# Attention and a two-layer ffn in one kernel: the switch to TensorE's written order at tile 39 instead of tile 45

## The chip, the cores and the metric

The kernel runs on one core of a Trainium2 chip. The metric is the device time of one execution in microseconds. The kernel before took 706.51 us (median of 3 runs, 705.92 to 706.59).

## What is computed

The reference is an attention with a learned position bias, followed by a two-layer ffn on its output (shapes: 4 batches, 8 heads, 576 positions, head size 64; ffn 512 to 2048 to 512):

```python
scores = scale * np.matmul(q, k.transpose(0, 1, 3, 2))
...
h = np.maximum(x @ w1 + b1, 0.0)
bias = h @ w2
scores = scores + bias.transpose(2, 0, 1)[None, :, :, :]
...
attn = np.exp(scores)
attn = attn / (np.sum(attn, axis=-1, keepdims=True) + 1e-09)
return np.matmul(attn, v).astype(np.float32)
...
h = x @ w_in
relu6 = np.clip(h + 3.0, 0.0, 6.0)
g = h * relu6 / 6.0
return (g @ w_out).astype(np.float32)
```

The bias depends on positions and head alone, so it is the same for all batches.

## The kernel before, in words

**Attention.** The work of attention is cut into 144 tiles. A tile is one batch, one pair of heads and up to 128 query rows of one head. The first 64 tiles cover the query rows 0 to 255 of all batches, four tiles a unit (one batch, one pair of heads); the other 80 cover the rest, five tiles a unit. Each pass n of the main loop writes `front(n)` (L935) and `back(n)`: for tile n the score matmuls of the next tiles (`qk_step`, tile `s_ps`, L552, two tiles at once for the tiles from 32 on), the bias added with the row maximum (`soft_max`, DVE, L564), the exponential (ACT, L575), the split of the probabilities into two halves of 16 bits (`hl`, ACT or POOL L118 or L124, then DVE L141), their transpose by a DMA of the SP queue (`at`, L640), and, five tiles later, the product with v (`pv_ps`, L711).

**Bias table.** The table comes in 36 groups of 16 rows. A group is four relus (`z_e`, DVE L851 or ACT L855), eight matmuls (`b_ps`, L868), an eviction by ACT (`bo`, L884) and a store to memory (L890), from where the tiles load it again.

**Ffn.** There are eight ffns, one for each batch and each half of the query rows; ffn(0, 0) is the first. Each is a generator of steps. Sixteen h steps of 12 matmuls each (`h_ps`, L786) are followed for each step by a relu on ACT (L776), a multiply on DVE (L769), a 16-bit copy on ACT (L763) and a subtraction on POOL (L765). Sixteen o steps of 12 matmuls each (`o_ps`, L809) follow, with one eviction by ACT (`ot`, L819) for every four. Of the first ffn the o steps also wait for w_out, which is unpacked on the chip.

**What sets the order.** Up to a switch, a scheduler sets the order of all engines' instructions. At the switch, `open_steady` (L1132) writes all that is left of ffn(0, 0), calls `open_banks` (L1126), and calls `keep_order("PE")` (L1099), after which TensorE's instructions stand as the program writes them. `open_banks` changes the PSUM places from three double places for `s` and two single ones for `w` to two and four (`open_psum`, L73). With the four `w` places the bias matmuls go to two `w` places instead of one `s` place, and their eviction becomes two instructions of 288 columns instead of one of 576 (`bias_mm` L859, `bias_out` L874). After the switch the main loop gives each tile a credit of 2.0 ffn steps (key `rf`; 1.55 in the second half, key `rf1`) and writes steps as long as there is credit. Between the end of ffn(0, 0) and the switch the credit is kept but no step is written, because of the condition `(phase < 2 or steady[0])` (L1192). Here is the switch and the way it is called:

```python
    def open_steady():
        nonlocal phase
        while phase < 2:
            ffn_step()
        open_banks()
        steady[0] = True
        keep_order("PE")
...
        if n == START:
            open_ffn()
...
        if n == SWITCH:
            open_steady()
        if late:
            qk_step(n + 1)
```

Of the kernel before, what the change touches and what calls it, by code (L numbers as in the profile page):

```python
# [24 lines left out]
NG = S // 16  # L25
CQ = 2.0 ** -25
VC = 5 * 128
CFG = {'z0': 'AD', 'gz': 12, 'z1': 'AD', 'gz2': 16, 'zeng': 'DDA', 'sg': 'P', 'wm1': 'A', 'wm2': 'RRAAAAAA', 'hl': 'AP', 'gl': 'PP', 'vm': 'A', 'g0': 8, 'rwi': 2.0, 'rw0': 0.3, 'rw1': 0.7, 'ro': 0.85, 'rb': 1.7, 'rf0': 1.3, 'rf': 2.0, 'rf1': 1.55, 'la': 6, 'gq': 2, 'gap': 0.0, 'wu': 8, 'act': 'o', 'g1': 2, 'w64': 5, 'rfo': 2.3, 'tv': 'A', 'pw': 0, 'po': 0, 'gr': 'AD', 'wb': 3, 'fb': 2, 'spn': 45, 'sw': 45, 'ws': 2, 'kn': 10, 'kw': 1, 'os': 11, 'ro2': 2.0, 'bo': 12, 'rb0': 1.5, 'psw': 99, 'xp': 0, 'mw': 2}
F64_BIAS = 2.0 ** -112
F64_MAX = float(np.uint32(0x0FEFFFFF).view(np.float32))  # L30

# [2 lines left out]
def attention_moe_kernel(  # L34
# [16 lines left out]
    nc = tc.nc  # L51
    cfg = CFG
    tc.cur_priority = 10000
# [30 lines left out]
    phase = 0  # L84
    out_open = [False, 0]
    steady = [False]
    four = [False]
    queue = []
# [820 lines left out]
    def bias_next():  # L909
        z, m, o, d = emitted  # L910
        z_group(z)
        bias_mm(m)
        emitted[0] += 1
        emitted[1] += 1
        if o < m:
            bias_out(o)
            emitted[2] += 1
            bias_store()
# [16 lines left out]
    def front(n):  # L935
        late = at(n + 1) and not direct(*tiles[n + 1])
        if at(n + 1) and not late:
            qk_step(n + 1)
        if at(n):
            soft_max(n)  # L940
        if n == START:
            open_ffn()
        if n == cfg["psw"]:
# [5 lines that stand above are left out]
        if unit_at(n - 6):  # L949
            x_low(*unit_at(n - 6))  # L950
        if at(n - 1):
            soft_norm(n - 1)
        if at(n - 2):
            soft_low(n - 2)
            if tiles[n - 2][2] in (1, 3, 5, 7, 8):
                freed[0] += 1
        if at(n):
            aux(n)
        if at(n - 3):
            soft_turn(n - 3)  # L960
        if unit_at(n - 5):
            pv_step(*unit_at(n - 5))
        while len(bt_t) - freed[0] < 4 and len(bt_t) < len(keys):
            k, b, p, i = keys[len(bt_t)]
            if k - n > (cfg["la"] if n > 3 else 2):
                break
            bias_until(128 * i + 128 if i < 2 else S)
            bt_t[b, p, i] = load_bias(b, p, i)
        if unit_at(n - 6) and unit_at(n - 6)[1] == PAIRS - 1:
            return unit_at(n - 6)[::2]  # L970
        return None

    def back(n):
        if unit_at(n - 5):
            x_high(*unit_at(n - 5))
        if at(n):
            soft_exp(n)
# [83 lines left out]
    def steps(gen, acc, rate):  # L1061
        acc[0] += rate
        while acc[0] >= 1.0:
            acc[0] -= 1.0
            next(gen, None)
# [28 lines left out]
    credit = 0.0  # L1094
# [4 lines left out]
    def keep_order(*names):  # L1099
        engines = {getattr(mybir.EngineType, e) for e in names}  # L1100
        in_order.enter_context(tc.manual_schedule(engines=engines))
# [40 lines left out]
    def out_step():  # L1142
        if next(gen_o, "end") == "end":
            return False
        out_steps[0] += 1
        return True

    def ffn_step():
        nonlocal phase
        r = next(queue[0], "end")  # L1150
        if r == "w2":
            phase = 1.5
        if r == "end":
            queue.pop(0)
            phase = 2
        return r != "end" and r != "w2"
# [9 lines left out]
    for n in range(-1, NT + 7):  # L1166
        for _ in range(cfg["g1"]):
            if emitted[0] < 16:
                bias_next()
        if n < 7:  # L1170
            next(gen_v, None)
        if n == cfg["spn"]:
            keep_order("SP")
        done = front(n)
        if phase == 0:
            steps(gen_w, aw, cfg["rw1"])
        else:
            ao[0] += cfg["ro"] if out_steps[0] < cfg["os"] else cfg["ro2"]
            while ao[0] >= 1.0:
                ao[0] -= 1.0  # L1180
                out_ready = not out_step()
        if phase and out_steps[0] >= cfg["bo"]:
            steps(gen_b, ab, cfg["rb"])
        if done is not None and done != (0, 0):
            b, u = done
            queue.append(ffn(b, u))
        if queue:
            if phase == 1.5 and not out_ready:
                credit = cfg["gap"]
            else:  # L1190
                credit += cfg["rf0"] if phase == 1 else cfg["rfo"] if phase < 2 else cfg["rf1" if unit_no[min(n, NT - 1)] >= 16 else "rf"]
            while credit >= 1.0 and queue and (phase < 2 or steady[0]):  # L1192
                if ffn_step():
                    credit -= 1.0
                if phase == 1.5 and not out_ready:
                    break
        back(n)
# [8 lines left out]
def _layout(q, k, v, w1, b1, w2, moe_w_in, moe_w_out):  # L1206
# [7 lines left out]
    qkd = _np.concatenate([kd, qd], axis=5).reshape(Bn, PAIRS, 2, 128, HALF + 256)  # L1214
    qkd = qkd.transpose(0, 1, 3, 2, 4).reshape(Bn, PAIRS, 128, 512 + S)[:CFG["fb"]]
    rows = _np.arange(128)[:, None] + 128 * _np.arange(5)[None, :]
# [44 lines left out]
```

## Time and profile before

| | us |
|---|---|
| median of 3 runs | 706.51 |
| the profiled execution, its own time | 703.41 |
| its span, first to last instruction | 701.6 |
| TensorE matmul busy | 643.9 (92%) |
| VectorE busy | 485.6 (69%) |
| ScalarE busy | 488.1 (70%) |
| GpSimd busy | 261.8 (37%) |
| granted TensorE clock, mean | 0.981 of 2.4 GHz |

Busy time is the union of an engine's instructions over the span. TensorE's is the largest, but it is an average over stages: what the change is worth has to be read in the stretch between the new place of the switch and the old one. The granted clock is a mean of two levels, 1.2 and 2.4 GHz.

### The profile page before, as it was taken

Reading aid. Unit: us, or ns where it says so; the run is one execution under the profiler, and the core shown is the slowest. Engines: PE = TensorE matmul, PEld = TensorE weight load, DVE = VectorE, ACT = ScalarE, POOL = GpSimd, SP = SyncE. Lnnn points to the kernel's source line nnn. Section 1 sums busy time; section 2 is a strip of 40 time slices with the busy share of each in tenths; the row PEclk is TensorE's granted clock in tenths of the full one; section 3 lists DMA queues with packets and bytes.
Section 4 is the critical chain, followed back from the end, with each engine's and each line's share of the span. In section 5 each row is a group of like instructions: output and inputs, shape, how many; then the busy total and the mean of one; then the engine's idle time right before and its main releaser. Section 6 shows DMA issues by size and latency. Waiting matters only on the chain. (4 is left out here: it accounts for less than half of the span.)

```text
span 701.6 us, 15111 instructions
## 1 busy us (share of the span) xinstructions
PE 643.9 (92%) x5558; PEld 455.8 (65%) x5558; DVE 485.6 (69%) x1157; ACT 488.1 (70%) x963; POOL 261.8 (37%) x322
## 2 busy tenths in 40 slices
PE   7687899775997999899899799999999999999998
PEld 2234456552673777687788688767777777777775
DVE  7989878899758577568778877887678767610310
ACT  7987778986846788678658866887578756721620
POOL 1112126765202443147435643564245522520420
PEclk9989999998999899999999999999999999999999
DMA  8899679644897938998899899978895877300000
GB/s 295 294 349 340 244 291 341 235 138 105 222 232 189 244 71 222 219 260 185 211 241 258 166 184 198 226 135 187 166 221 135 192 139 148 56 10 29 1 10 28
DMA packets 175738, 130.13 MB, mean 185 GB/s; under 512 B 137521, under 2 KB 144945, under 8 KB 174641
## 3 DMA queue, kind: packets, MB, share of 16 engines
q1 hardware_dynamic: 165872, 113.84, 64.9%
q10 hardware_dynamic: 9792, 15.34, 7.2%
q8 instruction: 43, 0.70, 0.4%
q14 instruction: 31, 0.25, 0.1%
HBM read 77.24 MB, written 15.34 MB: 132 GB/s over the span
## 5 line engine op out<-in xcount | busy, mean ns | idle before, releaser
L786 PE MATMUL h_ps<-x,wi 128*128 128x256 f16 (+1 forms) x1536 | 200.1, 288 | 6.8 <-DVE x L141 3.3
L809 PE MATMUL o_ps<-g,wo 128*128 128x256 f16 (+1 forms) x1536 | 196.0, 286 | 1.1 <-POOL g L765 1.1
L786 PEld LDWEIGHTS <-wi 128*128 128x128 f16 x1536 | 147.9, 98 | 55.3 <-issue 12.9
L809 PEld LDWEIGHTS <-wo 128*128 128x128 f16 x1536 | 147.2, 98 | 47.7 <-issue 10.6
L765 POOL TENSOR_TENSOR g<-t,g 128x256 f16<-128x256 f32 (+1 forms) x128 | 104.2, 825 | 123.6 <-ACT g L763 122.9
L575 ACT ACTIVATE bt<-bt,sm 128x576 f32<-128x576 f32 x144 | 110.9, 771 | 53.2 <-DVE sm L564 51.6
L141 DVE SCALAR_TENSOR_TENSOR hl<-bt,sm,hl 128x576 f16<-128x576 f32 x112 | 99.7, 902 | 27.6 <-ACT hl L124 15.0
L769 DVE SCALAR_TENSOR_TENSOR t<-t,t,h_ps 128x320 f32<-128x320 f32 (+1 forms) x112 | 56.2, 516 | 66.0 <-ACT t L776 64.7
L118 POOL TENSOR_SCALAR hl<-bt,sm 128x576 f16<-128x576 f32 x56 | 46.7, 834 | 94.4 <-DVE sm L587 39.2
L763 ACT ACTIVATE g<-t 128x256 f16<-128x256 f32 (+1 forms) x128 | 55.6, 441 | 35.5 <-DVE t L769 34.6
L418 POOL TENSOR_TENSOR qkl<-st,qkh 128x576 fp32r<-128x576 f32 (+2 forms) x48 | 61.1, 1293 | 38.0 <-ACT qkh L411 31.0
L564 DVE CUSTOM_DVE_ANT_0 bt<-s_ps,bt 128x576 f32<-128x576 f32 x88 | 64.6, 751 | 14.4 <-PE s_ps L552 7.9
L776 ACT ACTIVATE t<-h_ps,t,hr 128x320 f32<-128x320 f32 (+1 forms) x112 | 64.6, 588 | 8.6 <-PE h_ps L786 6.9
L868 PE MATMUL b_ps<-z_e,w_sb 128*32 128x288 f32 x448 | 47.2, 440 | 17.0 <-POOL x L699 7.5
L819 ACT ACTIVATE ot<-o_ps,os 128x256 f32<-128x256 f32 (+1 forms) x32 | 16.0, 499 | 56.5 <-PE o_ps L809 55.6
L124 ACT ACTIVATE hl<-bt,sm 128x576 f16<-128x576 f32 x56 | 43.1, 772 | 10.5 <-issue 3.0
L583 DVE TENSOR_SCALAR sm<-sm 128x1 f32<-128x1 f32 x112 | 16.8, 150 | 41.2 <-ACT bt L575 41.2
L851 DVE TENSOR_SCALAR z_e<-T,nbp 128x576 f32<-128x576 f32 x69 | 38.8, 608 | 2.6 <-PE b_ps L868 2.5
L868 PEld LDWEIGHTS b_ps<-z_e,w_sb 128*32 128x32 f32 x448 | 15.4, 114 | 37.4 <-DVE z_e L851 8.0
L552 PE MATMUL s_ps<-qkh 64*128 64x288 f32 x192 | 30.0, 349 | 8.3 <-ACT bo L884 5.0
L855 ACT ACTIVATE z_e<-T,bp 128x576 f32<-128x576 f32 x43 | 32.4, 770 | 6.8 <-PE b_ps L868 3.1
L258 POOL TENSOR_SCALAR w<-w 128x1024 f32<-128x1024 f32 x8 | 11.5, 1441 | 64.0 <-ACT wo L257 57.9
(132 smaller groups left out, 908.6 us busy)
## 6 DMA issues: line engine op xcount, KB each, us to landing
bt<-bias SPq DMA_DIRECT2D x36, 576.0 KB, 5.7
bias<-bo ACTq DMA_DIRECT2D x36, 288.0 KB, 5.4
w<-in_w_in_dram SPq DMA_DIRECT2D x8, 1024.0 KB, 7.1
vs<-in_vp_dram SPq DMA_DIRECT2D x24, 320.0 KB, 5.4
st<-in_qk_dram SPq DMA_DIRECT2D x16, 448.0 KB, 4.5
wo<-in_w_out_dram SPq DMA_DIRECT2D x5, 1024.0 KB, 6.4
bt<-bias SPq DMA_DIRECT2D x16, 288.0 KB, 3.5
qk<-in_qkd_dram SPq DMA_DIRECT2D x8, 544.0 KB, 8.9
```

Of the source, the lines that this page charges most:

```text
L118: nc.gpsimd.tensor_scalar(out=out, in0=full, scalar1=scale, scalar2=1.0, op0=ALU.mult, op1=ALU.mult)
L141: nc.vector.scalar_tensor_tensor(out=out, in0=full, scalar=scale, in1=high, op0=ALU.mult, op1=ALU.subtract)
L418: nc.gpsimd.tensor_sub(out=lo[:, c:c + w], in0=t[:, c:c + w], in1=hi[:, c:c + w].bitcast(F32))
L564: nc.vector.tensor_tensor_reduce(out=halves(bt), in0=ps, in1=halves(src), op0=ALU.add, op1=ALU.min, scale=-0.125, scalar=3.0e38, accum_out ...
L575: nc.scalar.activation(out=bt, in_=bt, func=AF.Exp, scale=-1.0, bias=sm[:, 0:1], accum_out=total)
L763: nc.scalar.activation(out=g[:, 0], in_=uu, func=AF.Copy)
L765: e.tensor_sub(out=g[:, 1], in0=uu, in1=g[:, 0])
L769: nc.vector.scalar_tensor_tensor(out=t_t[f], in0=t_t[f], scalar=cols(f)[2], in1=h_t.pop(f)[:, 0:n], op0=ALU.min, op1=ALU.mult,)
L776: nc.scalar.activation(out=t_t[f], in_=h_t[f][:, 0:n], func=AF.Relu, scale=cols(f)[0], bias=cols(f)[1],)
L786: nc.tensor.matmul(out=h_t[f][:, 0:n], lhsT=wi[:, a, c, f * 128:(f + 1) * 128], rhs=x[:, e, c], start=(k == 0), stop=(k == 3 * KC - 1),)
L809: nc.tensor.matmul(out=ops[:, 0:n], lhsT=wo[:, a, f, e * 128:(e + 1) * 128], rhs=g_t[f][:, r], start=(f == 0 and a == 0 and r == 0), stop= ...
L868: nc.tensor.matmul(out=pss[a][32 * k:32 * k + 32, 0:HALF], lhsT=w2_sb, rhs=z[:, a * HALF:(a + 1) * HALF],)
```

## The change

One number of the table at the top, `sw`, goes from 45 to 39. It is `SWITCH`, the tile at which `open_steady` is called. A new key `he` is 0, so the condition that names it is what it was.

```diff
-CFG = {... 'spn': 45, 'sw': 45, 'ws': 2, ... 'mw': 2}
+CFG = {... 'spn': 45, 'sw': 39, 'ws': 2, ... 'mw': 2, 'he': 0}
...
-            while credit >= 1.0 and queue and (phase < 2 or steady[0]):
+            while credit >= 1.0 and queue and (phase < 2 or steady[0] or cfg["he"]):
```

The number moves instructions on all engines but SP, whose order stays the same row for row. The first place is TensorE around the scores of tiles 44 to 47. Before, these rows stand there (`b_ps` is a group of the bias table, `m_ps` a step of the scale of v, `s_ps` the scores; a row's last number is how many follow each other):

```order
L868 MATMUL b_ps<-z_e,w_sb 32x288 x7
L157 MATMUL m_ps<-g_v_2299,ones_sb 128x1
L552 MATMUL s_ps<-qkh 128x288 x2
L552 MATMUL s_ps<-qkl,qkh 128x288 x2
L552 MATMUL s_ps<-qkh,qkl 128x288 x2
L868 MATMUL b_ps<-z_e,w_sb 32x288 x16
L552 MATMUL s_ps<-qkh 128x288 x4
L552 MATMUL s_ps<-qkl,qkh 128x288 x4
L552 MATMUL s_ps<-qkh,qkl 128x288 x4
L868 MATMUL b_ps<-z_e,w_sb 32x288 x8
L786 LDWEIGHTS wi
L786 MATMUL h_ps<-x,wi 128x256
```

Nothing of an ffn stands between the scores of tiles 44 and 45 (three rows of two matmuls, the second half of a pair that the scheduler had split) and those of 46 and 47 (three rows of four). The last row is the first of 120 matmuls of `h_ps`, ten steps that are written at once. With the change, the scores of a pair stand so (this is tiles 42 and 43, the rows of the following pairs are alike):

```order
L786 LDWEIGHTS wi
L786 MATMUL h_ps<-x,wi 128x256
L552 MATMUL s_ps<-qkh 128x288 x4
L552 MATMUL s_ps<-qkl,qkh 128x288 x4
L552 MATMUL s_ps<-qkh,qkl 128x288 x4
L153 MATMUL m_ps<-eye_sb,m_v_2275 1x128
L868 MATMUL b_ps<-z_e,w_sb 32x288 x8
L786 LDWEIGHTS wi
L786 MATMUL h_ps<-x,wi 128x256
```

The h steps of ffn(1, 0) now stand in pieces of 24 matmuls between the scores, the bias groups and the products with v, from the pair of tiles 40 and 41 on. Between the last o step that both orders share and the scores of tiles 48 and 49, TensorE had 84 matmuls of `o_ps`, the scores of four pairs, seven bias groups, two products with v and 144 matmuls of `h_ps`; it now has the same with 192 of `h_ps`. From there to the end the new order is 48 ffn matmuls ahead of the old one at the same tile (60 at some tiles), and after the last product with v 528 of them are left instead of 576.

The second place is ScalarE, which evicts and converts for all of these. Before, around the same tiles (`vh` is a half of v, `qkh` a half of q and k):

```order
L124 ACTIVATE vh<-vs,s_v_1309 128x640
L890 DMA bias_99<-bo 16x8x576
L124 ACTIVATE hl<-bt,sm 128x576
L855 ACTIVATE z_e<-T,bp 128x576
L884 ACTIVATE bo<-b_ps,cv_sb,isc 128x576
L890 DMA bias_100<-bo 16x8x576
L411 ACTIVATE qkh<-st 128x832
L575 ACTIVATE bt,sm<-bt,sm 128x576
L884 ACTIVATE bo<-b_ps,cv_sb,isc 128x288
```

And with the change:

```order
L884 ACTIVATE bo<-b_ps,cv_sb,isc 128x288
L575 ACTIVATE bt,sm<-bt,sm 128x576
L776 ACTIVATE t<-h_ps,t_1745,hr_2230 128x256
L890 DMA bias_99<-bo 16x8x576
L884 ACTIVATE bo<-b_ps,cv_sb,isc 128x288
L776 ACTIVATE t<-h_ps,t_1745,hr_2230 128x256
L124 ACTIVATE hl<-bt,sm 128x576
L855 ACTIVATE z_e<-T,bp 128x576
L884 ACTIVATE bo<-b_ps,cv_sb,isc 128x288
L855 ACTIVATE z_e<-T,bp 128x576
L763 ACTIVATE g<-t 128x256
L776 ACTIVATE t<-h_ps,t_1745,hr_2230 128x256
```

The relus and copies of the h steps (L776, L763) now stand among the evictions of the bias groups, which come in halves of 288 columns. In all, 32 evictions are halves instead of 22, and 20 are whole instead of 25.

## Rows read from the trace of the kernel before

**Rows 1.** The chain that ended last, in order of time: start, us, what.

```profile
460.56 1.06 PE s_ps L552 x7
...
617.87 2.02 PE pv_ps L711 x28
...
672.16 26.09 PE o_ps L809 x192
```

**Rows 2.** Windows: length, busy us of PE, PEld, DVE, ACT, POOL; clock, DMA, GB/s.

```profile
197.27:251.03 53.76, 47.27 (x451) 34.33 (x447) 34.49 (x83) 36.99 (x70) 15.40 (x20) 0.94 0.78 205
...
251.03:311.90 60.87, 58.74 (x627) 43.90 (x628) 41.25 (x97) 45.95 (x93) 19.10 (x24) 1.00 0.86 202
...
311.77:334.00 22.23, 20.76 (x217) 17.25 (x217) 17.86 (x43) 19.02 (x45) 14.66 (x20) 1.00 0.84 203
```

**Rows 3.** Timeline of TensorE, 218 to 234 us: start, us, what [idle before <-releaser].

```profile
218.71 1.94 PE L868 MATMUL b_ps<-z_e,w_sb 128*32 128x288 f32 x16
222.17 2.02 PE L868 MATMUL b_ps<-z_e,w_sb 128*32 128x288 f32 x16 [1.53 <-DVE z_e L851]
224.12 0.40 PE L552 MATMUL s_ps<-qkh 64*128 64x288 f32 x1
229.48 0.84 PE L552 MATMUL s_ps<-qkh 64*128 64x288 f32 x3 [4.97 <-ACT bo L884]
...
231.22 2.15 PE L868 MATMUL b_ps<-z_e,w_sb 128*32 128x288 f32 x16
233.29 13.98 PE L786 MATMUL h_ps<-x,wi 128*128 128x256 f16 x120
```

**Rows 4.** Timeline of all engines, ScalarE's rows before 229 us.

```profile
227.26 0.78 ACT L124 ACTIVATE hl<-bt,sm 128x576 f16<-128x576 f32 x1 [2.14 <-DMA at<-hl]
...
228.62 0.81 ACT L884 ACTIVATE bo<-b_ps,cv_sb,isc 128x576 f32<-128x576 f32 x1
```

**Rows 5.** Timeline of TensorE, 199 to 217 us, without waits.

```profile
199.99 0.53 PE L552 MATMUL s_ps<-qkh 64*128 64x288 f32 x4
...
200.98 1.18 PE L868 MATMUL b_ps<-z_e,w_sb 128*32 128x288 f32 x16
202.09 5.41 PE L809 MATMUL o_ps<-g,wo 128*128 128x256 f16 x48
207.43 1.17 PE L711 MATMUL pv_ps<-at,vh 128*64 128x256 f16 x18
...
209.09 1.48 PE L809 MATMUL o_ps<-g,wo 128*128 128x256 f16 x12
...
212.59 0.27 PE L153 MATMUL m_ps<-eye_sb,m_v 128*1 128x128 f32 x1
...
215.05 0.53 PE L552 MATMUL s_ps<-qkh 64*128 64x288 f32 x2
...
216.03 1.40 PE L868 MATMUL b_ps<-z_e,w_sb 128*32 128x288 f32 x14
```

**Rows 6.** Window of ffn(1, 0)'s h steps before, columns as in rows 2.

```profile
233.29:262.33 29.04, 29.04 (x296) 23.15 (x293) 19.12 (x43) 24.29 (x53) 12.96 (x20) 0.97 0.57 145
```

**Rows 7.** ScalarE's groups by line in that window: xcount | busy us, mean ns.

```profile
L884 ACT ACTIVATE bo<-b_ps,cv_sb,isc 128x288 f32<-128x288 f32 x6 | 3.5, 582 | 0.0
L855 ACT ACTIVATE z_e<-T,bp 128x576 f32<-128x576 f32 x4 | 3.1, 770 | 0.0
L575 ACT ACTIVATE bt<-bt,sm 128x576 f32<-128x576 f32 x3 | 2.3, 769 | 0.3 <-DVE sm L564 0.3
L124 ACT ACTIVATE hl<-bt,sm 128x576 f16<-128x576 f32 x2 | 1.5, 766 | 0.0
...
L124 ACT ACTIVATE vh<-vs,s_v 128x640 f16<-128x640 f32 x1 | 0.8, 832 | 0.1
```

**Rows 8.** Windows of 10 us: the one with ScalarE's largest share after 250 us.

```profile
390.00:400.00 10.00, 8.10 (x87) 6.58 (x87) 8.50 (x19) 9.37 (x22) 7.72 (x10) 1.00 0.67 134
```

**Rows 9.** Timeline of TensorE, the longest wait of a bias group after 250 us.

```profile
291.31 1.17 PE L868 MATMUL b_ps<-z_e,w_sb 128*32 128x288 f32 x12 [2.13 <-ACT z_e L855]
```

More of the change, by code (lines that the diff above doesn't have):

```diff
@@ L27 @@
 VC = 5 * 128
-CFG = {'z0': 'AD', 'gz': 12, 'z1': 'AD', 'gz2': 16, 'zeng': 'DDA', 'sg': 'P', 'wm1': 'A', 'wm2': 'RRAAAAAA', 'hl': 'AP', 'gl': 'PP', 'vm': 'A', 'g0': 8, 'rwi': 2.0, 'rw0': 0.3, 'rw1': 0.7, 'ro': 0.85, 'rb': 1.7, 'rf0': 1.3, 'rf': 2.0, 'rf1': 1.55, 'la': 6, 'gq': 2, 'gap': 0.0, 'wu': 8, 'act': 'o', 'g1': 2, 'w64': 5, 'rfo': 2.3, 'tv': 'A', 'pw': 0, 'po': 0, 'gr': 'AD', 'wb': 3, 'fb': 2, 'spn': 45, 'sw': 45, 'ws': 2, 'kn': 10, 'kw': 1, 'os': 11, 'ro2': 2.0, 'bo': 12, 'rb0': 1.5, 'psw': 99, 'xp': 0, 'mw': 2}
+CFG = {'z0': 'AD', 'gz': 12, 'z1': 'AD', 'gz2': 16, 'zeng': 'DDA', 'sg': 'P', 'wm1': 'A', 'wm2': 'RRAAAAAA', 'hl': 'AP', 'gl': 'PP', 'vm': 'A', 'g0': 8, 'rwi': 2.0, 'rw0': 0.3, 'rw1': 0.7, 'ro': 0.85, 'rb': 1.7, 'rf0': 1.3, 'rf': 2.0, 'rf1': 1.55, 'la': 6, 'gq': 2, 'gap': 0.0, 'wu': 8, 'act': 'o', 'g1': 2, 'w64': 5, 'rfo': 2.3, 'tv': 'A', 'pw': 0, 'po': 0, 'gr': 'AD', 'wb': 3, 'fb': 2, 'spn': 45, 'sw': 39, 'ws': 2, 'kn': 10, 'kw': 1, 'os': 11, 'ro2': 2.0, 'bo': 12, 'rb0': 1.5, 'psw': 99, 'xp': 0, 'mw': 2, 'he': 0}
 F64_BIAS = 2.0 ** -112
```

## The prediction

> **What bounds the kernel now.** I read the chain of waits first. From 460 us to the end it is TensorE alone, with hardly a gap: the scores at 460.56, the last product with v at 617.87, then only ffn matmuls, the last 192 of them in 26.09 us [rows 1]. So whatever TensorE does not get done before 460 us is paid at the end, at full price, and a microsecond that TensorE loses before then is a microsecond of the total. The question is how much it loses where the change works.
>
> The windows answer this. Between the last o step that both orders share (197.27 us) and the scores of tiles 48 and 49 (251.03 us) lie 53.76 us, of which TensorE is busy 47.27; the mean granted clock is 0.94, so part of it runs at 1.2 instead of 2.4 GHz. In the 60.87 us behind it TensorE idles 2.13 us, and the clock is 1.00 [rows 2]. The timeline shows the place: a bias group waits 1.53 us for VectorE's `z_e`, then the second score matmul of tiles 46 and 47 waits 4.97 us for ScalarE's eviction `bo`, because bias group and scores share the three `s` places; the rows after it take about twice their price until 233.29, where 120 matmuls of `h_ps` follow [rows 3]. ScalarE itself was late there: it stood 2.14 us before `hl`, for a transpose by DMA, with `bo` queued two instructions behind [rows 4]. TensorE had nothing else to do, as its order holds no ffn work between tiles 44 and 47.
>
> **The change, step by step.** First the prices, as distances between starts: the scores of a pair 0.99 us (199.99 to 200.98), a bias group 1.11, 48 matmuls of `o_ps` 5.34 (0.111 each), a product with v 1.66, a step of the v scale 0.27 [rows 5]; 120 matmuls of `h_ps` take 13.98, 0.1165 each [rows 3].
>
> *What TensorE must do in the stretch.* Before: 84 o matmuls 9.35, four pairs of scores 3.96, seven bias groups 7.77, two products with v 3.32, two small matmuls 0.54, 144 h matmuls 16.78; the sum is 41.7. It took 53.76 [rows 2], so 12.0 us are lost: 6.5 idle, and the rest the low clock and a pair of scores that the scheduler had split, whose half alone takes 0.98 (215.05 to 216.03) [rows 5]. With the change the same list has 192 h matmuls, 5.6 us more, 47.3 in all: without any wait, tiles 48 and 49 would be reached at 244.6 instead of 251.0, with 48 ffn matmuls more behind them. At the end, 48 matmuls less are left, 6.5 us by the last 192 (26.09 / 192 = 0.136 each) [rows 1]. Both are one gain: the total falls by what of the 12.0 us is no longer lost.
>
> *What is lost anew in that stretch: 5.0 us.* The h steps now run beside the bias groups, and ScalarE serves both. From the first h matmul (197.27 + 9.35 + 0.99 + 1.11 = 208.7) to 244.6 TensorE has 35.9 us of work. Before, the same sixteen h steps stood in a window of 29.04 us in which ScalarE was busy 24.29 [rows 6]. Counted in the order, the new stage has beside these 8 more half evictions (4.7 us at 582 ns), 4 more `z_e` (3.1), 5 more exponentials (3.8), 2 more `hl` (1.5) and 3 more conversions of the size of `vh` (2.5) [rows 7]. That makes 39.9 us of ScalarE for 35.9 of TensorE, so it falls 4.0 behind even if it never waits. The lower bound of the loss is the share that TensorE idles in the window after 251.03, 2.13 of 60.87, which is 1.3 us [rows 2]; the upper one is the densest 10 us of ScalarE, 9.37 busy, where TensorE gets 8.10 [rows 8]: 35.9 / 0.81 is 44.3, a loss of 8.4. I take 5.0, nearest the deficit itself.
>
> *What moves on from there: 1.0 us.* Two bias groups now fall into the h steps of the next ffn, which had none. That stage is 22.23 us with ScalarE at 19.02 [rows 2]; two groups are four half evictions and two or three `z_e`, 4.2 us, so 23.2 us, a deficit of 1.0. The bounds are 0 (ScalarE catches up in the o steps that follow) and 4.2.
>
> *Edits counted at nothing.* SP's order does not move. The reset of the PSUM places costs nothing that the order shows: it comes behind the drained o steps, whose last eviction is ScalarE's alone, and the next scores need only places that were read long before. If that cover is gone, it is one eviction, under 1 us. The two `s` places make a pair of scores wait for both row maxima of the pair before; with h steps between the pairs that is hidden, as it is after 251.03 now. Scores of tiles 40 and 41 start 60 o matmuls later than before (6.7 us), which hurts only if attention becomes the bound; it is ahead again by tiles 48 and 49.
>
> The sum is 12.0 - 5.0 - 1.0 = 6.0 us. Against the profiled execution, whose own time is 703.41 for a span of 701.6, that gives a span of 695.6 and an own time of 697.4. The median of the runs, 706.51, lies 3.1 above the profiled one; I carry the difference over: **700.5 us**.
>
> **The rivals.** A change under 1.4 us (0.2%) can't be told from none.
>
> *ScalarE takes the hole back.* If it sets the pace of the whole stage as in the densest 10 us, the loss is 8.4 us and the next stage adds 2.0, the middle of its bounds: 706.5 - 1.6 = 704.9, and 707.1 with 4.2 for the next stage. For it: the 39.9 against 35.9 above. Against: ScalarE has little to do during the o steps before 208, and its order puts relus between the bias rows. In this direction points a rule of the Trainium skill, "Perfetto Trace Analysis", section "Identifying the Most-Contended Engine": judge TensorE by its weight loads' share and not by matmul time, and take the engine with the highest share as the one to work on. By it the h window reads 23.15 for weight loads and 24.29 for ScalarE of 29.04 [rows 6], so ScalarE is the bound there and another order of TensorE gains nothing: 706.5. The trace speaks against it in that window, since TensorE's matmuls fill all 29.04.
>
> *Slower: a wait at each bias group.* TensorE's written order is rigid: behind each group's eight matmuls stand 24 h matmuls that can't pass it. After 250 us one group waited 2.13 us for ScalarE's `z_e` [rows 9]. If all seven in the stretch do, 14.9 us are lost where 12.0 were, and with the 1.0 of the next stage the time is 706.5 + 3.9 = 710.4. It decides from a mean of 1.6 us a group, (12.0 - 1.0) / 7. For it: relus and copies now stand ahead of `z_e` on ScalarE. Against: nine groups stand in the 60.87 us after 251.03, in written order, and all idle time of TensorE there is 2.13 us [rows 2].
>
> *The hole is filled for nothing.* ScalarE keeps up and TensorE loses as little as after 251.03, or later waits shrink as well: up to 12.0 us less, 694.5.
>
> *The change doesn't do what it says.* The credit could have been spent elsewhere; but the order shows the 48 matmuls ahead from tile 48 to the end. It would be 706.5.
>
> **How the numbers follow.** The forecast, 696.5 to 703.5, gets 0.62: the hole is in rows, its cause (no ffn work there) goes, and the deficit of ScalarE is smaller than the hole. The hole taken back gets 0.16, of which 0.09 lies below 705.1 and 0.07 about 706.5; the hole for nothing 0.13; slower 0.07; no effect 0.02. So faster is 0.62 + 0.13 + 0.09 = 0.84, the same 0.07 + 0.02 = 0.09, slower 0.07. The range is 696.0 to 705.0: the forecast and the near halves of the two cases beside it, with the dearest ScalarE loss (8.4 us and little behind it) still in it.
>
> **What would show it.** Right: no wait of TensorE over 3 us between 197 and 250 us, and the clock near 1.00 there; the scores of tiles 48 and 49 about 1.4 us earlier, near 249.6; ScalarE over 90% busy between 209 and 249, with short waits of `h_ps` and `b_ps` for ScalarE or VectorE that add up to some 5 us; the last product with v within 1 us of 617.9, and 528 ffn matmuls instead of 576 behind it, 6.5 us less. Wrong: a new wait of several us in the stretch, followed by rows at twice their price, or an idle time after 251.03 that grows by more than 2 us, which would mean that attention and not TensorE sets the pace.

## The result, and the profile after

| | before | changed |
|---|---|---|
| median, us | 706.55 (6 runs, 705.24 to 707.76) | 698.59 (6 runs, 696.51 to 700.03) |
| profiled execution, own time | 703.41 | 696.51 |
| its span | 701.6 | 694.5 |
| granted TensorE clock, mean | 0.981 | 0.990 |

The ratio is 0.9887, with a 95% interval of 0.9862 to 0.9912: the change makes the kernel 8.0 us faster. Forecast were 700.5 us, in a range of 696.0 to 705.0.

In the first part of the changed kernel's page the busy times of VectorE, ScalarE and GpSimd are those of before within 0.5 us; TensorE's matmuls have 5.7 us less (643.9 before):

```profile
PE 638.2 (92%) x5558; PEld 453.0 (65%) x5558; DVE 485.6 (70%) x1157; ACT 487.7 (70%) x968; POOL 261.7 (38%) x322
```

No matmul was taken away. So the gain has to be looked for in waits, and in matmuls that ran at the higher clock. The windows of the changed kernel answer to [rows 2]; columns as there.

```profile
200.96:251.92 50.96, 48.52 (x499) 36.08 (x495) 36.48 (x87) 40.26 (x83) 18.43 (x24) 1.00 0.73 199
251.92:311.90 59.98, 57.81 (x619) 43.32 (x619) 41.15 (x95) 44.46 (x92) 19.10 (x25) 1.00 0.95 214
```

The first window is the stretch of the prediction, from the last shared o step to the scores of tiles 48 and 49. It is 2.8 us shorter than before (53.76) and holds 48 more matmuls of the ffn, which are worth 5.6 us. TensorE idles 2.4 us in it instead of 6.5, and the clock is 1.00 instead of 0.94. The second window is much as before: 2.17 us idle, where it was 2.13.

TensorE's timeline, 200 to 252 us, against [rows 3] and [rows 5] (start, us, what, idle before and its releaser in brackets):

```profile
200.96 9.34 PE L809 MATMUL o_ps<-g,wo 128*128 128x256 f16 x84
210.23 0.53 PE L552 MATMUL s_ps<-qkh 64*128 64x288 f32 x4
...
212.33 2.79 PE L786 MATMUL h_ps<-x,wi 128*128 128x256 f16 x24
...
226.13 0.69 PE L868 MATMUL b_ps<-z_e,w_sb 128*32 128x288 f32 x8 [0.38 <-DVE p_v L160]
...
245.38 2.30 PE L868 MATMUL b_ps<-z_e,w_sb 128*32 128x288 f32 x16 [0.28 <-ACT z_e L855]
249.21 2.78 PE L786 MATMUL h_ps<-x,wi 128*128 128x256 f16 x24 [1.52 <-DVE t L769]
251.92 0.54 PE L552 MATMUL s_ps<-qkh 64*128 64x288 f32 x4
```

The wait of 4.97 us before the scores of tiles 46 and 47 is gone; nothing waits longer than 1.52. The waits that the profile lists for TensorE in this stretch, by what ended them (total us, times, longest):

```profile
PE h_ps L786 <- DVE t L769: 1.5, 1, 1.5
PE b_ps L868 <- DVE p_v L160: 0.4, 1, 0.4
PE b_ps L868 <- ACT z_e L855: 0.3, 1, 0.3
PE h_ps L786 <- ACT bo L884: 0.3, 1, 0.3
```

The chain that ended last, its tail, against [rows 1] (start, us, what):

```profile
617.23 2.02 PE pv_ps L711 x28
619.25 19.67 PE o_ps L809 x144
638.92 26.08 PE h_ps L786 x192
665.00 26.09 PE o_ps L809 x192
```

The last product with v starts at 617.23, where it was 617.87, and behind it stand 144 + 192 + 192 = 528 ffn matmuls instead of 576. Here the gain reaches the end of the kernel: 48 matmuls less, 6.5 us, plus the 0.64.

### The profile page after: what moved, and what is told of

Read it like the earlier page. It is cut to its first block, busy times and chain, and to the rows that moved or that the text cites. A ratio compares the mean times of both kernels' runs of the same rounds, so it can differ in the third digit from the quotient of the medians.

```text
span 694.5 us, 15117 instructions
## 1 busy us (share of the span) xinstructions
PE 638.2 (92%) x5558; PEld 453.0 (65%) x5558; DVE 485.6 (70%) x1157; ACT 487.7 (70%) x968; POOL 261.7 (38%) x322
## 5 line engine op out<-in xcount | busy, mean ns | idle before, releaser
L141 DVE SCALAR_TENSOR_TENSOR hl<-bt,sm,hl 128x576 f16<-128x576 f32 x112 | 99.1, 896 | 20.8 <-POOL hl L118 12.8
L763 ACT ACTIVATE g<-t 128x256 f16<-128x256 f32 (+1 forms) x128 | 55.4, 439 | 36.3 <-DVE t L769 35.5
L418 POOL TENSOR_TENSOR qkl<-st,qkh 128x576 fp32r<-128x576 f32 (+2 forms) x48 | 58.5, 1238 | 37.5 <-ACT qkh L411 30.3
L776 ACT ACTIVATE t<-h_ps,t,hr 128x320 f32<-128x320 f32 (+1 forms) x112 | 64.3, 586 | 7.2 <-PE h_ps L786 2.9
L868 PE MATMUL b_ps<-z_e,w_sb 128*32 128x288 f32 x448 | 45.4, 430 | 15.3 <-POOL x L699 5.9
L851 DVE TENSOR_SCALAR z_e<-T,nbp 128x576 f32<-128x576 f32 x69 | 40.9, 638 | 1.9 <-PE b_ps L868 1.7
L884 ACT ACTIVATE bo<-b_ps,cv_sb,isc 128x288 f32<-128x288 f32 (+1 forms) x52 | 35.0, 674 | 4.3 <-DMA bias<-bo 2.4
```

What stands on the lines that cost most here:

```text
L141: nc.vector.scalar_tensor_tensor(out=out, in0=full, scalar=scale, in1=high, op0=ALU.mult, op1=ALU.subtract)
L418: nc.gpsimd.tensor_sub(out=lo[:, c:c + w], in0=t[:, c:c + w], in1=hi[:, c:c + w].bitcast(F32))
L763: nc.scalar.activation(out=g[:, 0], in_=uu, func=AF.Copy)
L776: nc.scalar.activation(out=t_t[f], in_=h_t[f][:, 0:n], func=AF.Relu, scale=cols(f)[0], bias=cols(f)[1],)
L868: nc.tensor.matmul(out=pss[a][32 * k:32 * k + 32, 0:HALF], lhsT=w2_sb, rhs=z[:, a * HALF:(a + 1) * HALF],)
```

## The experiments

Two theories stood against each other at first. **Filling**: the gain comes from ffn work that stands between attention's matmuls in the stretch, so that TensorE has something to do while a bias group waits for its relus. **Places** or **order**: it comes from the PSUM places or from TensorE's written order, which the change also moves to tile 39. The first four runs take the change apart. For each run I work out from its profile what its stretch lost: its length, less the work in it by the prices of [rows 5] and [rows 3] (41.7 us with 144 h matmuls, 47.3 with 192). Before it was 12.0 us.

**Only the PSUM places at tile 39** (the key `psw` calls `open_banks` there; the rest of the switch stays at 45):

```diff
-'sw': 45, ... 'psw': 99
+'sw': 45, ... 'psw': 39
```

> Edit: only the PSUM places change at tile 39 (two double, four single); TensorE's written order and the further ffns still open at tile 45. Filling theory (the gain comes from h steps that stand where TensorE had nothing to do): no ffn work moves, so 705.0 to 708.0, and a stretch without ffn work between the scores of tiles 44 and 48 is still there. Places theory (the 4.97 us wait for the eviction of a bias group in a shared place was the loss): that wait goes, about 5 us and the low clock behind it come back, 698.5 to 701.5.

Measured: 708.89 us beside 706.68, ratio 1.0031 (1.0010 to 1.0052), slightly slower, and 0.9 above the range of the filling theory. TensorE's timeline in its stretch, with one row of ScalarE:

```profile
232.35 0.65 PE L868 MATMUL b_ps<-z_e,w_sb 128*32 128x288 f32 x2 [0.73 <-DVE z_e L851]
...
234.87 0.77 ACT L124 ACTIVATE hl<-bt,sm 128x576 f16<-128x576 f32 x1 [2.44 <-DMA at<-hl]
...
237.32 2.14 PE L868 MATMUL b_ps<-z_e,w_sb 128*32 128x288 f32 x14 [4.33 <-ACT z_e L855]
239.40 14.02 PE L786 MATMUL h_ps<-x,wi 128*128 128x256 f16 x120
```

The hole is still there, 4.33 us, though the bias group no longer shares places with the scores. It waits for the relu `z_e` now. So the three shared `s` places, which the prediction named as the hole's cause, were only the place where the lateness showed: with nothing of the ffn to do, TensorE meets the bias groups' relus and evictions wherever they are late. Lost: 13.7 us. The lateness itself begins further up, at the same place as before [rows 4]: ScalarE stood 2.44 us before `hl`, for a transpose by DMA, and this `z_e` was queued behind it. In the changed kernel's stretch ScalarE has no such wait. No run moves the transposes alone, so what makes them late is open.

**Only the written order from tile 39:**

```diff
+        if n == 39:
+            keep_order("PE")
...
     def open_steady():
...
-        keep_order("PE")
```

> Edit: only TensorE's written order begins at tile 39; places and further ffns at tile 45. Filling theory: no ffn work moves, but the pair of scores that the scheduler had split is whole again (1.0 us), so 704.5 to 707.5, with the hole between the scores of tiles 44 and 48. Order theory (the scheduler's order itself cost the time): 698.5 to 701.5.

Measured: 707.03 us beside 706.68, ratio 0.9999 (0.9980 to 1.0018). No effect, and the same hole:

```profile
233.78 2.15 PE L868 MATMUL b_ps<-z_e,w_sb 128*32 128x288 f32 x16 [4.71 <-ACT bo L884]
235.85 15.04 PE L786 MATMUL h_ps<-x,wi 128*128 128x256 f16 x120
```

**Places and order at tile 39, but no ffn steps until tile 45:**

```diff
     def open_steady():
...
-        steady[0] = True
...
+        if n == 45:
+            steady[0] = True
```

> Edit: places, written order and the end of ffn(0, 0) at tile 39 as in the change, but steps of further ffns are written from tile 45 only (14 at once, so from tile 48 on the counts are those of the change). Filling theory: the four pairs of scores from tile 40 to 47 stand without ffn work between them, the hole stays or grows, 705.0 to 709.0. Places or order theory: 698.5 to 701.5, as the change.

Measured: 707.53 us beside 706.68, ratio 1.0009 (0.9982 to 1.0037). This is the change without its ffn steps, and nothing of the gain is left; 13.0 us are lost, with waits of 2.03 and 3.00 us:

```profile
220.01 3.40 PE L868 MATMUL b_ps<-z_e,w_sb 128*32 128x288 f32 x16 [2.03 <-DVE z_e L851]
...
234.66 3.31 PE L868 MATMUL b_ps<-z_e,w_sb 128*32 128x288 f32 x16 [3.00 <-ACT z_e L855]
237.90 18.80 PE L786 MATMUL h_ps<-x,wi 128*128 128x256 f16 x168
```

The groups behind these waits took 3.40 and 3.31 us where one takes 1.18 undisturbed.

**Only the ffn steps early** (no new places, no written order):

```diff
-'sw': 45, ... 'mw': 2
+'sw': 45, ... 'mw': 2, 'he': 1
```

> Edit: only the further ffns open early (as soon as ffn(0, 0) has ended), in the scheduler's order and with the old places until tile 45. 60 matmuls of h_ps then stand between the scores of tiles 42 and 47 instead of behind them; from tile 48 on the counts are those of the kernel before. Filling theory: up to 7.0 us of work fills the hole (6.5 us idle and the low clock), ScalarE gives back some 2, so 700.0 to 703.5. Places and order theories: 705.0 to 708.0, since neither moves.

Measured: 704.19 us beside 706.68, ratio 0.9971 (0.9951 to 0.9990), a quarter of the gain and between the two ranges expected. Its longest waits now end with the multiply `t` of an h step:

```profile
229.47 1.47 PE L786 MATMUL h_ps<-x,wi 128*128 128x256 f16 x12 [0.53 <-DVE t L769]
234.45 2.19 PE L786 MATMUL h_ps<-x,wi 128*128 128x256 f16 x12 [2.38 <-DVE t L769]
...
243.60 0.69 PE L868 MATMUL b_ps<-z_e,w_sb 128*32 128x288 f32 x8 [0.61 <-DVE t L769]
```

An h step waits until VectorE's multiply `t` has read the `w` place that it needs, and there are only two, which the products with v and the steps of the v scale use as well. So filling alone fell short, and a third theory came up: the ffn steps need the four `w` places, or the written order, or both. The next two runs add one of these each; the change itself ran beside them.

> The change itself once more, on the chip of the three runs beside it, as their measure. All theories: 697.0 to 700.5.

The change again: 698.03 us beside 707.17, ratio 0.9864 (0.9832 to 0.9896). Its stretch, in the windows:

```profile
198.65:249.65 51.00, 48.56 (x500) 36.09 (x497) 36.44 (x87) 40.30 (x83) 18.44 (x24) 1.00 0.76 193
```

The length repeats to 0.04 us (50.96 and 51.00), though the stretch starts 2.3 us earlier in this execution.

**Ffn steps and written order, old places:**

```diff
-'sw': 45, ... 'mw': 2
+'sw': 45, ... 'mw': 2, 'he': 1
...
+        if n == 39:
+            keep_order("PE")
...
     def open_steady():
...
-        keep_order("PE")
```

> Edit: the further ffns open early and TensorE's written order begins at tile 39, but the PSUM places stay (three double, two single) until tile 45. 96 h matmuls stand in pieces of 24 between the scores, as in the change; from tile 48 on the counts are those of the kernel before. Filling alone (it is enough that h steps stand there in written order): 699.0 to 702.0. Filling needs the four single places (with two, each h step waits for VectorE's multiply of the step before the last, as in the run with the ffns alone, where such waits were 2.38, 0.53 and 0.61 us): 702.5 to 705.5.

Measured: 706.19 us beside 707.17, ratio 0.9983 (0.9958 to 1.0007), 0.7 us above the higher of the two ranges. TensorE's timeline:

```profile
220.68 2.72 PE L786 MATMUL h_ps<-x,wi 128*128 128x256 f16 x12 [3.46 <-DVE t L769]
...
234.32 1.17 PE L711 MATMUL pv_ps<-at,vh 128*64 128x256 f16 x18 [1.68 <-DVE t L769]
...
248.48 2.78 PE L786 MATMUL h_ps<-x,wi 128*128 128x256 f16 x24 [1.52 <-DVE t L769]
```

With two `w` places and an order in which nothing may pass the waiting h step, the hole of 4.97 us before the scores is exchanged for 3.46 and 1.68 us before an h step and a product with v; 9.8 us are lost. The wait of 1.52 us does not come from the places: the change has it too.

**Ffn steps and new places, the scheduler's order:**

```diff
-'sw': 45, ... 'psw': 99, ... 'mw': 2
+'sw': 45, ... 'psw': 39, ... 'mw': 2, 'he': 1
```

> Edit: the further ffns open early and the PSUM places change at tile 39, but the scheduler sets TensorE's order until tile 45 (h steps in pieces of 12, scores of pairs split). Filling needs the places and not the written order: 699.0 to 702.0. Filling needs the written order: 703.0 to 706.0.

Measured: 700.40 us beside 707.17, ratio 0.9886 (0.9849 to 0.9923): most of the gain without the written order, 2.4 us above the change beside it, with intervals that overlap. Its stretch:

```profile
200.80:247.71 46.91, 46.08 (x451) 33.02 (x447) 34.96 (x84) 37.00 (x74) 15.32 (x19) 1.00 0.85 202
```

TensorE idles 0.8 us. What else this run loses by the prices lies in its busy time: the scheduler leaves four halves of score pairs apart, and a half takes as long as a pair (0.98 us [rows 5]), some 2 us together. So the gain needs two of the three parts, each of which alone gives little or nothing: ffn steps in the stretch, and four single `w` places for them and the bias groups. Of the Trainium skill's "Perfetto Trace Analysis", section "Optimization Strategy", two rules can be held against these runs. Where regimes with different limits follow each other, interleaving them may help: the trace agrees, since the run without interleaved ffn steps lost 13.0 us and the change 3.7. And a gap that repeats can mean that there are too few buffers: the trace agrees here too, with two places 3.46 and 1.68 us behind `t`, with four one wait of 1.5.

**The switch at tile 42**, to see whether the gain grows with the tiles that are filled:

```diff
-'sw': 45
+'sw': 42, ... 'he': 0
```

> Edit: the switch at tile 42. The h steps stand between the scores of tiles 44 to 48 with four single places; from tile 48 on the counts are those of the kernel before, so the tail is not shorter by a matmul. Filling theory (the gain is the time that TensorE no longer loses, wherever the counts end): 698.5 to 702.0. Rival (the gain is the 48 matmuls that the change takes out of the tail): 705.0 to 708.0.

Measured: 704.02 us beside 707.17, ratio 0.9950 (0.9924 to 0.9976), between the two expectations; neither foresaw why. TensorE's timeline:

```profile
218.62 0.38 PE L157 MATMUL m_ps<-g_v,ones_sb 1*128 1x1 f32 x2 [3.59 <-DVE sm L583]
...
220.04 7.03 PE L786 MATMUL h_ps<-x,wi 128*128 128x256 f16 x48
```

Here the written order puts a tiny matmul of the v scale ahead of a bias group and 48 h matmuls. It waits 3.59 us for VectorE, they wait with it, and then the h matmuls take 7.03 us instead of 5.6 (48 by 0.1165). Of the gain 3.5 us are left. A written order is worth as much as the instruction in front.

**Does ScalarE bind what is left?** The prediction put the remaining loss down to ScalarE. The split `hl` goes to ScalarE for every second tile and to GpSimd for the others. Two runs move it, for tiles 40 to 49 of the changed kernel, all to GpSimd, and all to ScalarE:

```diff
-        return pick("hl", n)
+        return "P" if 40 <= n < 50 else pick("hl", n)
```

> Edit, on the change: the first half of the probabilities of tiles 40 to 49 (hl) is made by GpSimd alone instead of ScalarE and GpSimd in turn, so ScalarE has 5 conversions of 0.77 us less (3.9 us) in the stretch. If ScalarE is what still costs TensorE time there (3.7 us are lost with the change): 1 to 2.5 us faster than the change, 695.5 to 697.5, and the stretch 1 to 2.5 us shorter. If ScalarE does not bind: as the change, 697.5 to 699.0.

```diff
-        return pick("hl", n)
+        return "A" if 40 <= n < 50 else pick("hl", n)
```

> Edit, on the change: hl of tiles 40 to 49 by ScalarE alone, 5 conversions more (3.9 us). If ScalarE, 93% busy there, binds: 2 to 4 us slower than the change, 700.0 to 702.5, and the stretch longer by as much. If it does not bind: 697.5 to 699.0.

Measured: 698.32 us (ratio 0.9878, 0.9847 to 0.9909) with GpSimd, 699.06 (0.9893, 0.9866 to 0.9920) with ScalarE, both beside 707.11. Windows of the run with GpSimd, the stretch and 6.31 us near its end (ACT is the fourth engine):

```profile
200.38:251.71 51.33, 48.75 (x499) 36.07 (x495) 36.80 (x88) 38.12 (x79) 23.07 (x27) 1.00 0.77 200
...
242.69:249.00 6.31, 4.86 (x44) 3.02 (x41) 5.18 (x13) 6.31 (x14) 4.52 (x5) 1.00 1.05 289
```

The stretch of the run with ScalarE:

```profile
199.58:251.88 52.30, 48.20 (x500) 36.16 (x496) 36.23 (x87) 42.45 (x87) 14.89 (x19) 1.00 0.75 196
```

Taking 2.1 us from ScalarE (40.26 to 38.12) does not shorten the stretch (51.33 against 50.96 and 51.00). Adding 2.2 us (to 42.45) lengthens it by 1.3, less than the 2 to 4 expected; the totals can't be told apart. So the sum of ScalarE's work over the stretch does not set the 3.7 us. The second window is the place where most of them are lost, as shown below: ScalarE has no idle time in it, here as in the change. The easing made it 0.6 us shorter, and new waits of 0.45 and 0.25 us for `t` further up in this run took that back.

**The switch earlier still**, at tile 38 and 37:

```diff
-'sw': 45
+'sw': 38, ... 'he': 0
```

> Edit: the switch at tile 38; 72 ffn matmuls ahead instead of 48. Filling theory: there is no hole left to fill, only some of the 3.7 us, so 696.5 to 699.5. Rival (each ffn matmul taken out of the tail is gained): 24 x 0.136 = 3.3 us more, 694.0 to 695.5.

```diff
-'sw': 45
+'sw': 37, ... 'he': 0
```

> Edit: the switch at tile 37; 96 ffn matmuls ahead. Filling theory: 696.5 to 700.5, slower if the o steps of the first ffn, now written right behind the unpacking of w_out, wait for it in order. Rival: 6.5 us more than the change, 691.0 to 692.5.

Measured beside 707.11: 697.85 us (ratio 0.9867, 0.9843 to 0.9891) and 696.25 us (0.9852, 0.9823 to 0.9882), the second 0.25 under the range of the filling theory and 3.75 above the rival's. Behind the last product with v, 120 and then 84 o matmuls stand ahead of the last two blocks of 192, where the change has 144. The tail of the chain at tile 38:

```profile
624.07 16.41 PE o_ps L809 x120
640.48 26.08 PE h_ps L786 x192
666.56 26.09 PE o_ps L809 x192
```

and at tile 37:

```profile
627.73 11.52 PE o_ps L809 x84
639.24 26.08 PE h_ps L786 x192
665.32 26.09 PE o_ps L809 x192
```

The tails are 24 and 60 matmuls shorter than the change's, 3.3 and 8.2 us at 0.136, but they begin 4.8 and 8.5 us later than its 619.25. So matmuls that are done earlier are not won by themselves; what is won is the waits that they fill. The fastest median of all is that of tile 37, but its interval and the change's overlap.

The stretch accounts for all these totals. What each run gained in its stretch (12.0 less what it lost) against what it gained in all (706.9, the mean of the medians of the kernel before, by one less its ratio). The switches at 38 and 37 are not in the table, since they move work across the start of the stretch:

| run | ffn steps, places, order at 39 | lost in the stretch | gained there | gained in all |
|---|---|---|---|---|
| only places | -, yes, - | 13.7 | -1.7 | -2.2 |
| only order | -, -, yes | 12.8 | -0.8 | 0.1 |
| places and order | -, yes, yes | 13.0 | -1.0 | -0.6 |
| only ffn steps | yes, -, - | 9.3 | 2.7 | 2.0 |
| ffn steps and order | yes, -, yes | 9.8 | 2.2 | 1.2 |
| ffn steps and places | yes, yes, - | 5.2 | 6.8 | 8.1 |
| the change, twice | yes, yes, yes | 3.7, 3.7 | 8.3, 8.3 | 8.0, 9.6 |
| switch at 42 | from 42 on | 8.3 | 3.7 | 3.5 |
| change, `hl` on GpSimd | yes, yes, yes | 4.0 | 8.0 | 8.6 |
| change, `hl` on ScalarE | yes, yes, yes | 5.0 | 7.0 | 7.6 |

## Why the prediction was right, point by point

**The bound, and the 12.0 us.** Right. The prediction said that a microsecond that TensorE loses before 460 us is one of the total, and the table shows it: over eleven profiles the last two columns agree within 1.4 us.

**The hole and its cause.** The hole was right, its cause half right. That no ffn work stood there is shown by the run that keeps places and order and leaves the ffn steps where they were. That bias group and scores share the `s` places is not the cause: with `w` places for the bias the hole was 4.33 us. The transposes that kept ScalarE waiting, which the prediction read in [rows 4], stood ahead of that hole too. What the prediction did not say is that the four `w` places are a condition. It counted the reset of the places at nothing; as a cost that holds, but without it the change would have brought 1 to 2 us instead of 8.

**The term of 5.0 us, lost anew.** This term was mis-sized, and its mechanism held at one place instead of over the stretch. It measured 3.7 us, in both profiles of the change. The prediction worked out 39.9 us of ScalarE work for 35.9 of TensorE. From the first h matmul to the scores of tiles 48 and 49, and in the place near the end where two bias groups come close together, the changed kernel's windows are

```profile
212.33:251.92 39.59, 37.15 (x387) 26.70 (x383) 33.79 (x82) 36.88 (x78) 18.43 (x24) 1.00 0.70 179
...
242.31:249.21 6.90, 5.09 (x44) 3.02 (x41) 5.69 (x15) 6.90 (x16) 4.10 (x5) 1.00 1.05 334
```

In the first, ScalarE was busy 36.88 of 39.59 us, which is 3.0 us less work than counted; so either the count was too high, or some of it ran later. The second lies between the starts of two pieces of 24 h matmuls. TensorE's work in it is one such piece, 2.8 us by the price, and a bias group of 1.11; the other 3.0 of its 6.90 us are lost, out of 3.7 in the whole stretch. Of these 1.52 are the wait for `t`, and 1.1 lie inside the bias group at 245.38, which took 2.30 us instead of 1.18 at a clock of 1.00. ScalarE is busy in all 6.90 us, with exponentials and relus in turn, and VectorE waits for it:

```profile
247.27 0.15 DVE L583 TENSOR_SCALAR sm<-sm 128x1 f32<-128x1 f32 x1 [1.18 <-ACT bt L575]
247.34 1.37 DVE L851 TENSOR_SCALAR z_e<-T,nbp 128x576 f32<-128x576 f32 x3
...
248.70 0.46 DVE L769 SCALAR_TENSOR_TENSOR t<-t,t,h_ps 128x256 f32<-128x256 f32 x1
```

VectorE stands 1.18 us before `sm`, for ScalarE's exponential, with three rows of `z_e` and the multiply `t` queued behind it; `t` ends at 249.16, and the 24 h matmuls that waited 1.52 us for it start at 249.21. So ScalarE does fall behind, as predicted, but over 7 us, in part through VectorE's queue, and not by the sum of its work over 36 us: easing the stretch by 2.1 us shortened this place by 0.6 and the stretch by nothing. One run has another order here. With the switch at tile 37, o matmuls of the ffn follow the slow group:

```profile
250.79 2.30 PE L868 MATMUL b_ps<-z_e,w_sb 128*32 128x288 f32 x16 [0.41 <-ACT z_e L855]
253.02 2.79 PE L809 MATMUL o_ps<-g,wo 128*128 128x256 f16 x24
```

They start without a wait, and this kernel has the lowest median, 1.8 us under the 698.03 of the change. But more than this place differs in it, and the intervals overlap, so it is not shown that the wait of 1.52 us can be won in full.

**The term of 1.0 us in the next stage.** It came out on either side of nothing. The part from the scores of tiles 48 and 49 to the last product with v has the same work before and after, since the 48 matmuls are ahead at both ends. Before, it took 366.84 us (617.87 - 251.03). The change's first profile has 365.31 (617.23 - 251.92), the second 367.77 (617.42 - 249.65), so 1.5 less and 0.9 more. Two places tell the two profiles apart, a wait and a window (the granted clock is its third number from the end). The first profile:

```profile
291.18 1.17 PE L868 MATMUL b_ps<-z_e,w_sb 128*32 128x288 f32 x12 [1.60 <-ACT z_e L855]
...
343.00:347.00 4.00, 3.67 (x49) 3.21 (x50) 3.00 (x12) 3.58 (x8) 0.91 (x3) 1.00 1.10 320
```

and the second, with its last product with v:

```profile
290.09 1.16 PE L868 MATMUL b_ps<-z_e,w_sb 128*32 128x288 f32 x12 [2.53 <-ACT z_e L855]
...
343.00:347.00 4.00, 4.00 (x37) 3.13 (x37) 3.28 (x9) 3.56 (x8) 0.75 (x1) 0.60 1.32 271
...
617.42 2.02 PE pv_ps L711 x28
```

One wait for `z_e` is 0.9 us longer, and at 343 us the granted clock was 0.60, where the first profile had 1.00 and the one before 0.62. This makes up the 2.5 us between them: 1.6 of it lie between two neighbouring pairs of scores (343.33 to 350.00 in the first, 341.91 to 350.15 in the second). Two executions of one kernel differ here by more than the term, so its size stays open.

**The sum.** The prediction took 48 matmuls as 5.6 us in the stretch and 6.5 in the tail, called both one gain, and counted that gain by the 5.6. So its sum leaves out 0.9 us. The tail did get shorter by 6.5 (83.73 before, 77.27 and 77.28 after). From the start of the stretch to the end of the kernel the second profile gained 12.0 - 3.7 - 0.9 + 0.9 = 8.3 us and the first 12.0 - 3.7 + 1.5 + 0.9 = 10.7, against 6.0 forecast. The medians gained 8.0, and 9.6 by the ratio of the second set of runs. The 2 us between forecast and result are thus the 1.3 by which the term of 5.0 was too large and the 0.9 left out, and all else is within what executions differ by.

**The signs.** No wait over 3 us and a clock near 1.00 in the stretch: right. The last product with v within 1 us of 617.9, and 528 matmuls behind it: right. ScalarE over 90% busy between 209 and 249 us: 87% by these times (34.98 of 40.00 us), 93% from the first h matmul on, which came at 212.33. Waits that add up to some 5 us: they were 2.5, and 1.1 more inside one bias group. Scores of tiles 48 and 49 near 249.6: 251.92 in one profile and 249.65 in the other. This sign hung on the start of the stretch, ahead of which the instructions are the same, and that starts between 198.65 and 201.80 us in the other profiles here, but at 197.27 in the one of before. The length of the stretch was the sign to name.

**The rivals.** *A wait at each bias group*: of the seven groups, two waited, 0.38 and 0.28 us, and the second of these lost 1.1 us more within itself, far from the mean of 1.6 us that would have decided. *ScalarE takes the hole back* (704.9): ruled out by the time, and by a loss of 3.7 us where this rival needs 8.4. The rule of the Trainium skill beside that rival, "Perfetto Trace Analysis", section "Identifying the Most-Contended Engine", judges TensorE by its weight loads, 65% on the profile's page of the changed kernel, below ScalarE's and VectorE's 70%. The trace does not bear it out here: a change that left every other engine's busy time within 0.5 us gave a ratio of 0.9887 by removing lost time of TensorE, and 2.1 us less work for ScalarE in the stretch left the time where it was. *The hole filled for nothing* (694.5): not reached, 3.7 us stay. *No effect*: excluded by the interval.

## What to carry to other kernels

Price a hole in the bounding engine's stream by what could be written into it, and then ask where that work's results go: here the filler gave 2 us with two PSUM places and 8 with four, and the places alone gave nothing. Where several edits come as one, take them apart in pairs as well as singly, since run by themselves two of the three parts gave nothing and the third a quarter. And compare lengths between two instructions that both kernels have rather than moments of time, because the moments moved by several us from run to run where the instructions ahead were the same.

## What was not expected of the hardware

A small matmul can cost more than a large one. In the run with the switch at tile 42, two matmuls on 1x1 operands (0.38 us) held 48 others for 3.59 us, and these then took 7.03 us where 5.6 is their price. Their window shows the granted clock at 0.50, the lower of its two levels:

```profile
220.00:223.00 3.00, 3.00 (x18) 2.09 (x15) 3.00 (x9) 2.98 (x6) 1.21 (x1) 0.50 0.41 94
```

The kernel before has 0.50 behind its wait of 4.97 us as well (229 to 234 us), and so has the run without ffn steps around its wait of 2.03 us (218 to 224 us), where a bias group took 3.40 us against 1.18. Part of the 3.40 is waiting inside the group, since at the lower clock one took 2.15 [rows 3]. Behind the change's longest wait, 1.52 us, 24 h matmuls took 2.78 us at a clock of 1.00, their full-speed price. Which waits bring the clock down, these runs don't settle.

Executions of one kernel spread further than the gains of some parts: the kernel before gave 703.37 to 712.65 us over the 35 executions that stood beside the first four runs. Below about 1 us, only the medians of many runs could tell the parts apart.
